# One written order of all steps for a block-sparse attention with a cosine MLP, in place of a planner's priorities

## The chip, the cores and the metric

The kernel runs on one core of a Trainium2 chip. The time is the device time of one launch in microseconds; the median of three runs before the change is 837.22 us (833.31 to 837.58).

## What is computed

```python
def _attn_ref(q, k, v, sampled_blocks):            # q, k, v: (4, 8, 768, 64)
    scores = 1.0 / np.sqrt(D) * np.matmul(q, k.transpose(0, 1, 3, 2))
    mask = np.abs(blk_i - blk_j) <= 1              # blocks of 32 positions, 24 of them
    mask = mask | (blk_i == 0) | (blk_j == 0) | (blk_i == n_blocks - 1) | (blk_j == n_blocks - 1)
    for qb in range(n_blocks):
        for kb in sampled_blocks[qb]:              # three per block of queries
            mask[qb * 32:(qb + 1) * 32, kb * 32:(kb + 1) * 32] = True
    scores = np.where(mask, scores, -1000000000.0)
    attn = np.exp(scores - np.max(scores, axis=-1, keepdims=True))
    attn = attn / (np.sum(attn, axis=-1, keepdims=True) + 1e-09)
    return np.matmul(attn, v).astype(np.float32)

def _moe_ref(x, w_in, w_out):                      # x: 3072 x 512, d_ff 2048
    h = x @ w_in
    return ((h * np.cos(h)) @ w_out).astype(np.float32)
```

The attention's output, its heads side by side, is the x of the second part.

## The kernel before, in words

Work is cut into 24 query tiles of 128 positions, six per batch: five sparse ones (tiles 0 to 4, 6 to 10, 12 to 16, 18 to 22), in which the scores of a pair of heads cover 11 blocks each, and a dense one per batch (tiles 5, 11, 17, 23), which holds the first block and the last three and sees all keys, head by head. Two tiles make one of the 12 blocks of the MLP (block m is fed by tiles 2m and 2m + 1). Every float32 operand is split into a high and a low float16 part, and a product is three multiplications.

One tile goes through these steps, for each pair of heads (or each head of a dense tile): scores on TensorE (L1501, L1502, L1507; dense L1518), eviction with bias and maximum on VectorE (L1534), exponential on ScalarE (L1556), high and low part (ScalarE L1566, VectorE L1570), a transposing DMA of the probabilities that SyncE issues (L1585, PT<-ring; three PT buffers), and the value product on TensorE (L1595, L1607; dense L1621). Then the tile's output is normalised (VectorE L1643), split (L1645, L1647) and transposed by a DMA (L1650, xT<-n). A block of the MLP has, in each of four parts of d_ff, four up steps on TensorE (L1782, 12 multiplications each), evictions on ScalarE (L1791), the reduction of the argument on VectorE (L1801, L1805), the sine on ScalarE (L1809), the product (L1814), its high part (ScalarE L1820) and low part (VectorE L1823), and four down steps on TensorE (L1832, 6 multiplications each). In the first two blocks each part's result is added up on VectorE (L1848). An up or a down step is called an MLP step here. The exponential and the sine stand in different tables of ScalarE, so a change from one to the other is a table load.

Before a batch's first scores, its keys are loaded, squared (ScalarE L1237), reduced to one maximum over all partitions (VectorE L1275, TensorE L1282, VectorE L1285), split (ScalarE and VectorE L1251, L1254) and transposed by DMAs (L1337, W<-kn); its values are split likewise and stored to a scratch in DRAM (L1380), from which each tile's are gathered (SyncE L1460, L1463; GpSimd L1469). Queries are loaded (L1391), split, transposed (L1424) and their halves swapped (L1429, L1431). While the first tiles run, the weights are converted from float64 to float32 (L1693, L1695, L1697) and split (L1737, L1254).

plan_kernel writes down all 3202 steps, each with its engine, a cost, what it reads and writes, and a number pos. In Plan.run of before, a model of the engines, of two DMA queues and of TensorE's clock takes the steps one after the other: of those that could start soonest on an engine it picks the one with the least pos, plus a penalty for a change of table (TSTICK) or of the form of multiplication (MSTICK). A step that needs a new tile (class sp, P, ring, PT and so on, each with 1 to 4 buffers) gets the buffer that comes free soonest by the model. The order in which steps were taken is the order in which they are issued; each engine works through its own instructions in that order, and waits in place where an operand or a buffer isn't there.

Of the kernel before, what the change touches and what calls it, by code (L numbers as in the profile page):

```python
# [62 lines left out]
    -30.456, -29.801, -23.939, -53.034, 166.579, -20.984, 140.138, 219.885, 227.197, 131.714, 120.363, 232.646, -27.188, -24.922, -13.735, -56.138,  # L63
    -94, -55.947, 108.211, -77.198, -23.949, -53.212, -40.157, -72.798, 270.478, 66.707, 68.01, -177.497, 14.041, 28.322, 3.956, 272.798, -299.008,
    78.628, 84.172, -251.907, -2.914, -123.585, 2.465, -91.329, 2.455, 34.414, -267.676, -140.127, -284.431, -284.297, -293.381, -293.391, 192.593,
    9.365, -40.858, -287.926, -293.475, -287.096, 59.248, -394.248, -2.44, -348.918, 17.905, -232.784, 20.189, 100.731, -40.95, -331.99, -113.765,
    -40.634, -367.234, 46.043, -133.846, -367.224, 11.803, 4.97, 24.252, -421.344, 26.722, 28.591, 28.666, -343.265, 24.749, 57.069, 44.723, -158.181,
    36.406, -210.361, -15.746, -343.729, 128.652, -36.656, -371.38, -68.723, 16.426, -352.843, -40.021, 17.512, -383.377, -48.957, -21.419, -347.085,
    -28.841, 56.446, 43.124, 188.518, 11.424, -17.372, 21.646, 33.599, 92.429, 143.48, 196.289, -222.117, -122.398, 8.237, -189.078, -343.107,
    -342.925, 25.279, 10.938, -287.916, -291.521, -287.076, 58.942, 18.504, 18.357, -371.364, -101.311, -423.627, 74.946, -15.912, -13.582, 41.721,  # L70
    -245.857, -245.911, -244.196, -43.279, -222.107, -87.019, -399.291, -65.977, -134.438, 46.449, 60.7, 33.135, 4.468, 123.512, 268.427, 33.261,
    -248.251, -248.261, 212.998, -102.21, 48.096, 13.762, -106.375, -119.619, -147.859, -108.524, -207.38, 26.503, 77.242, -59.055, 1.603, 67.419,
    -87.097, -106.365, 67.989, -37.319, -59.065, 69.972, 72.05, -154.526, 55.53, -154.393, -169.552, 56.724, -229.085, -231.809, 74.109, 141.111,
    110.575, 115.939, -212.079, 38.276, 59.016, -125.91, 76.35, 74.089, 148.617, 164.638, -161.055, 83.947, 111.93, 81.411, 76.871, -59.456, -83.696,
    159.259, 85.519, 93.411, 17.344, 71.116, 184.532, 68.131, 74.808, 107.885, 77.651, 84.302, 130.956, 28.443, 113.94, 76.784, 109.173, 89.802,
    -45.113, 117.791, 159.783, 68.413, -124.822, -171.216, 43.388, 0.239, 17.471, -215.269, 120.448, 241.879, 122.369, 97.725, 62.454, 170.072,
    164.502, -7.94, -4.787, 2.973, -52.72, 223.723, 122.511, -117.03, -107.768, 171.807, 166.99, 31.038, -64.944, 122.176, -107.825, 122.166, 239.2,
    144.286, 112.315, 156.325, 382.871, 80.018, 71.115, -102.354, 162.701, -80.093, 79.039, -102.344, 99.128, 128.496, 58.997, -8.015, 105.462,
    35.675, -49.533, 145.181, 119.619, -28.145, 93.292, 142.357, 308.89, 128.763, 119.724, 117.514, 85.487, 85.477, 353, 135.215, 147.675, 191.49,
    174.352, -36.186, -36.871, -123.396, 176.099, -39.179, 309.094, -39.029, 132.778, 148.258, 163.293, -175.451, 70.065, 131.553, 172.196, -210.132,  # L80
    188.27, 242.828, 164.956, 160.647, -62.194, -92.423, 244.643, 165.526, -39.019, -40.767, -44.622, 45.727, 174.671, 176.081, 274.008, 148.864,
    212.867, -21.454, 198.526, 93.467, 88.563, 186.068, 198.293, 45.786, 47.752, -3.729, -25.778, -197.69, -62.453, -353.585, -65.75, -397.087, 40.03,
    -58.957, 41.172, 22.215, 6.449, 26.152, -152.555, 116.726, 144.461, 85.242, 267.182, -72.696, 32.61, -223.053, -234.241, -274.177, 88.133,
    -142.875, 36.777, -48.023, -48.508, -27.185, 36.777, -102.2, -105.699, -69.594, -75.188, -107.644, -166.721, 44.732, 50.054, 8.787, 37.825,
    -105.709, -42.273, -82.868, 10.422, -134.435, -66.455, 34.062, 91.891, 21.079, 56.89, -51.579, -9.933, 68.144, 253.555, -66.358, -348.47, 48.572,
    3.193, -182.808, -147.869, -130.834, 67.487, -210.07, 70.849, 1.538, 69.097, -108.251, 51.995, 60.727, -206.919, 14.069, -202.843, -210.687,
# [171 lines left out]
    604.774, 824.955, 1051.126, 942.72, 677.48, 454.761, 798.868, 681.849, 454.538, 686.552, 852.787, 839.193, 954.833, 823.585, 684.874, 898.166,  # L258
    688.133, 688.922, 863.203, 684.355, 688.932, 564.474, 873.725, 773.958, 800.794, 591.607, 799.478, 678.833, 688.123, 848.093, 681.039, 688.123,
    748.898, 735.298, 810.843, 809.183, 742.566, 703.148, 722.615, 732.095, 700.957, 675.385, 798.996, 569.188, 736.375, 735.308, 760.316, 655.823,  # L260
    635.618,
]


# [1649 lines left out]
```

## Time and profile before

| | |
|---|---|
| median of three runs | 837.22 us |
| profiled execution, its own time | 824.2 us |
| its span | 822.4 us |
| TensorE (PE) busy | 719.6 us, 87% |
| VectorE (DVE) busy | 641.1 us, 78% |
| ScalarE (ACT) busy | 635.7 us, 77% |
| GpSimd (POOL) busy | 107.4 us, 13% |
| mean granted TensorE clock | 0.938 |

Busy shares are averages over the whole span. The page cuts the span into 40 slices of 20.6 us, and a digit there is the busy share of one slice in tenths; PEclk is the granted clock of TensorE in the same way. The time between the span and the execution's own time is 1.8 us.

### The profile page before, as it was taken

The page shows a single profiled execution, that of the slowest core. Times are in us where ns is not written, and L with a number is a line of the kernel's source. Part 1 is how long each engine was busy: PE and PEld are TensorE (multiplying, and loading weights), DVE is VectorE, ACT ScalarE, POOL GpSimd, SP SyncE. Part 2 cuts the span into 40 slices and gives each one's busy share as a digit, 9 for nine tenths or more (in the row PEclk, how much of TensorE's full clock was granted, in tenths as well). Part 3 has the DMA queues.
Part 4 walks back from the last instruction along what each step waited for, and adds up shares of the span by engine and source line. Part 5 has one row for each costly group of instructions (what it writes and reads, how often), then busy time and mean ns, then how long its engine had stood idle before and what let it go on. Part 6 is the DMA issues. An engine that isn't in the chain of part 4 may idle for free.

```text
span 822.4 us, 23028 instructions
## 1 busy us (share of the span) xinstructions
PE 719.6 (87%) x9272; PEld 507.2 (62%) x9272; DVE 641.1 (78%) x1617; ACT 635.7 (77%) x1218; POOL 107.4 (13%) x128
## 2 busy tenths in 40 slices
PE   3537589899889856999999979999999979999998
PEld 2425467566466435767767647767586558577573
DVE  5979999999969763889878975989768957967362
ACT  3667899899868973999969985989679967977251
POOL 6232203000022022100030212000300210200000
PEclk9955689999899986999999998999999989999999
DMA  8999977954989899999997999978977997675100
GB/s 309 325 236 259 239 150 174 212 126 113 205 257 183 157 196 167 171 228 177 270 187 158 178 207 206 202 154 186 217 140 134 196 181 163 157 130 99 26 26 26
DMA packets 270299, 146.55 MB, mean 178 GB/s; under 512 B 241648, under 2 KB 241776, under 8 KB 270192
## 3 DMA queue, kind: packets, MB, share of 16 engines
q1 hardware_dynamic: 265072, 129.35, 74.3%
q0 software_dynamic: 5120, 15.73, 8.6%
q8 instruction: 72, 1.18, 0.6%
q14 instruction: 35, 0.29, 0.1%
HBM read 68.23 MB, written 12.58 MB: 98 GB/s over the span
## 4 chain that ended last, share of the span: by engine, by line
PE 37%; ACT 14%; DMA 13%; DVE 9%; issue 3%; SPq 1%; DVEq 0%; ACTq 0%
PE ph L1782 15%; PE po L1832 14%; DMA PT<-ring 7%; ACT P L1556 4%; PE xp L1607 2%; ACT ring L1566 2%; DMA W<-kn 2%; DMA scr<-n 2%; PE sp L1518 1%; DVE P L1534 1%; DMA qs<-in_q_dram 1%; ACT hs L1791 1%; DVE g L1823 1%; ACT junk L1237 1%; PE xp L1595 1%
## 5 line engine op out<-in xcount | busy, mean ns | idle before, releaser
L1782 PE MATMUL ph<-xT,w 128*128 128x256 f16 x2304 | 272.3, 277 | 8.3 <-ACT hs L1791 4.2
L1832 PE MATMUL po<-w,g 128*128 128x512 f16 x1152 | 265.6, 381 | 4.1 <-DVE kn L1848 1.6
L1782 PEld LDWEIGHTS <-w 128*128 128x128 f16 x2304 | 225.6, 99 | 45.6 <-issue 8.5
L1832 PEld LDWEIGHTS <-g 128*128 128x128 f16 x1152 | 108.7, 98 | 124.4 <-issue 4.1
L1556 ACT ACTIVATE P<-P,sm 128x352 f32<-128x352 f32 (+1 forms) x224 | 152.0, 680 | 32.3 <-DVE sm L1551 23.0
L1469 POOL DMA_INDIRECT V<-scr,gidx x80 | 91.8, 1147 | 595.0 <-PE xp L1595 278.2
L1570 DVE TENSOR_TENSOR ring<-P,ring 128x704 f16<-128x704 f32 (+1 forms) x112 | 100.5, 906 | 23.8 <-ACT ring L1566 22.7
L1534 DVE CUSTOM_DVE_ANT_1 P<-sp,bias 128x352 f32<-128x352 f32 x160 | 78.6, 519 | 35.4 <-PE sp L1507 35.1
L1791 ACT ACTIVATE hs<-ph,sm 128x512 f32<-128x512 f32 x96 | 63.0, 677 | 44.7 <-PE ph L1782 40.8
L1566 ACT CAST ring<-P 128x704 f16<-128x704 f32 (+1 forms) x112 | 86.5, 786 | 13.3 <-DMA PT<-ring 12.7
L1814 DVE SCALAR_TENSOR_TENSOR hs<-hs,sm,g 128x1024 f32<-128x1024 f32 x48 | 61.1, 1281 | 11.8 <-ACT g L1809 11.2
L1501 PE MATMUL sp<-W,U 128*128 128x192 f16 x320 | 52.5, 265 | 13.5 <-DVE sm L1534 10.7
L1823 DVE TENSOR_TENSOR g<-hs,g 128x1024 f16<-128x1024 f32 x48 | 58.6, 1223 | 6.9 <-ACT g L1820 6.8
L1809 ACT ACTIVATE g<-g,sm 128x1024 f32<-128x1024 f32 x48 | 54.7, 1145 | 11.5 <-DVE g L1805 11.2
L1595 PE MATMUL xp<-V,PT 96*32 96x64 f16 x1920 | 30.9, 203 | 35.4 <-DMA PT<-ring 35.4
L1805 DVE SCALAR_TENSOR_TENSOR g<-g,hs 128x1024 f32<-128x1024 f32 x48 | 58.3, 1218 | 0.6 <-DVE Wg L1343 0.2
L1820 ACT ACTIVATE g<-hs 128x1024 f16<-128x1024 f32 x48 | 50.4, 1051 | 8.4 <-DVE hs L1814 7.9
L1801 DVE TENSOR_SCALAR g<-hs 128x1024 f32<-128x1024 f32 x48 | 32.9, 690 | 28.0 <-ACT hs L1791 27.9
L1595 PEld LDWEIGHTS <-PT 96*32 96x32 f16 x1920 | 21.7, 102 | 51.7 <-DMA PT<-ring 43.5
L1502 PE MATMUL sp<-W,U 128*128 128x64 f16 x320 | 47.8, 205 | 0.0
L1607 PE MATMUL xp<-V,PT 128*128 128x64 f16 x960 | 46.6, 204 | 0.0
L1502 PEld LDWEIGHTS <-U 128*128 128x128 f16 x320 | 33.1, 104 | 15.5 <-issue 12.1
(164 smaller groups left out, 919.1 us busy)
## 6 DMA issues: line engine op xcount, KB each, us to landing
V<-scr SPq DMA_DIRECT2D x20, 384.0 KB, 5.1
stage<-in_k_dram SPq DMA_DIRECT2D x12, 512.0 KB
w<-in_moe_w_in_dram SPq DMA_DIRECT2D x12, 512.0 KB, 6.9
w<-in_moe_w_out_dram SPq DMA_DIRECT2D x12, 512.0 KB, 4.4
V<-scr SPq DMA_DIRECT2D x8, 768.0 KB, 6.3
scr<-n SPq DMA_DIRECT2D x21, 256.0 KB, 3.3
qs<-in_q_dram SPq DMA_DIRECT2D x20, 256.0 KB, 3.5
U<-U SPq DMA_DIRECT2D x40, 128.0 KB, 2.9
```

The lines of the kernel that those rows point to most:

```text
L1469: self.nc.gpsimd.indirect_dma_start(V[:96, 2 + j, :], None, self.scr[b][:, :], bass.IndirectOffsetOnAxis(ap=self.gidx[:96, c : c + 1], axi ...
L1502: mm(spv[:, :, 96:128].rearrange("p y (n c) -> p y n c", c=hf), u, ends, start=False, stop=False)
L1534: self.nc.vector.tensor_tensor_reduce(out=self.p_view(n, Pt)[:, a].rearrange("p (n c) -> p n c", c=hf), in0=sp[:, :w].rearrange("p (n c) - ...
L1556: self.nc.scalar.activation(Pv[:, a], Pv[:, a], AF.Exp, scale=qc[:, 4:5], bias=nb[:, bcol : bcol + 1], accum_out=sums[:, 2 * j + a : 2 * j ...
L1566: self.nc.scalar.copy(R[:, :, 0, : self.width(n)], self.p_view(n, Pt))
L1570: self.nc.vector.tensor_tensor(R[:, :, 1, :w], self.p_view(n, Pt), R[:, :, 0, :w], ALU.subtract)
L1607: mm(xp[:, h, :], PT[:, 6 * a + 3 * l + c, :], V[:, c, h, d0:d1], start=False, stop=(a == 1 and c == 1 and x == len(terms) - 1),)
L1782: self.nc.tensor.matmul(ph[:, ff, :], self.W1[p][:, wl, cc, c * P : (c + 1) * P], xT[:, xl * NCC + cc, :], start=(j == 0), stop=(j == len( ...
L1791: self.nc.scalar.activation(hs[:, h * 512 : h * 512 + 512], ph.rearrange("p f t -> p (f t)"), AF.Copy, scale=self.turns[b][:, p : p + 1])
L1814: self.nc.vector.scalar_tensor_tensor(hs, hs, c[:, p : p + 1], kt, op0=ALU.mult, op1=ALU.mult)
L1823: self.nc.vector.tensor_tensor(g[:, 1024:2048], hs, g[:, 0:1024], ALU.subtract)
L1832: self.nc.tensor.matmul(po, g[:, gl, ff, t * P : (t + 1) * P], self.W2[p][:, wl, ff, :], start=(first and ff == half * hf and j == 0), sto ...
```

## The change

The table POS holds a place in one total order for each of the 3202 steps (the whole numbers 0 to 3201) where it held priorities. Plan.run sorts the steps by it and issues them so, and no longer models times: ArrayClock and Queues are gone. A step's new tile gets a buffer that was never used, or else, of those whose last user already stands in the order, the one whose last use stands farthest back. The steps, their instructions and the number of buffers stay. Places in code behind the table differ by line only: a line of the changed kernel is the old one less 213 (L1432 was L1645).

```diff
 POS = [
-    -30.456, -29.801, -23.939, -53.034, 166.579, -20.984, 140.138, 219.885, 227.197, 131.714, 120.363, 232.646, -27.188, -24.922, -13.735, -56.138,
...
+    1, 11, 22, 12, 262, 52, 14, 3, 15, 80, 21, 105, 4, 17, 16, 18, 13, 29, 30, 31, 32, 33, 35, 37, 115, 323, 252, 40, 148, 92, 307, 609, 347, 179,
...
 ]
@@ Plan
-    def run(self, delta, stick, mstick=0.0):
...
-            for eng, cand in ready.items():
-                at = max(free[eng], dma.ends[0] - 1.75) if eng == "SP" else free[eng]
...
-                    key = (o.pos + (stick if o.table and o.table != table else 0.0) + (mstick if eng == "PE" and o.mode[0] != mode else 0.0), o.n)
...
-            for v in o.acq:
-                v.avail, v.slot = slot_time(v)
-                v.t = self.classes[v.cls][v.slot]
...
+    def run(self):
+        order = sorted(self.ops, key=lambda o: (o.pos, o.n))
+        for v in {id(v): v for o in order for v in o.acq}.values():
+            v.left, v.freed = len(v.ops), 0
             for o in v.ops:
                 o.vals.append(v)
         holder = {c: [None] * len(t) for c, t in self.classes.items()}
+        done = set()
+        for k, o in enumerate(order):
+            assert all(id(p) in done for p in o.preds | {v.ops[0] for v in o.held}), o.name
             for v in o.acq:
+                h = holder[v.cls]
+                free = [x for x in range(len(h)) if h[x] is None] or [x for x in range(len(h)) if not h[x].left]
+                x = min(free, key=lambda x: h[x].freed if h[x] else x)
+                h[x], v.t = v, self.classes[v.cls][x]
             for v in o.vals:
                 v.left -= 1
+                v.freed = k
+            done.add(id(o))
         self.order = order
@@ block_sparse_attention_then_cos_mlp
-    pl.run(PARAMS["DELTA"], PARAMS["TSTICK"], PARAMS["MSTICK"])
+    pl.run()
```

First piece: VectorE, where the keys of batch 1 are split and the first scores (tile 6, rows with bias) are evicted. kn is the split key, stage the loaded one, g and hs belong to block 2 of the MLP. Before:

```order
L1254 SCALAR_TENSOR_TENSOR kn1_89<-stage2_80,sm_77,kn1_89 128x4x64
L1254 SCALAR_TENSOR_TENSOR kn0_88<-stage1_79,sm_77,kn0_88 128x4x64
L1801 TENSOR_SCALAR g0_84<-hs1_83 128x1024
L1254 SCALAR_TENSOR_TENSOR kn1_89<-stage2_80,sm_77,kn1_89 128x4x64
L1805 SCALAR_TENSOR_TENSOR g0_84<-g0_84,hs1_83 128x1024
L1534 ISA P2_98,sm_77<-sp0_115,bias_74 128x352
L1534 ISA sm_77 128x1
L1534 ISA P2_98,sm_77<-sp0_115,bias_74 128x352
L1534 ISA sm_77 128x1
L1823 TENSOR_TENSOR g2_86<-hs0_82,g2_86 128x1024
L1551 TENSOR_SCALAR sm_77<-sm_77 128x2
```

After:

```order
L1041 SCALAR_TENSOR_TENSOR kn0_88<-stage3_81,sm_77,kn0_88 128x4x64 x2
L1321 ISA P2_98,sm_77<-sp0_115,bias_74 128x352
L1321 ISA sm_77 128x1
L1321 ISA P2_98,sm_77<-sp0_115,bias_74 128x352
L1321 ISA sm_77 128x1
L1338 TENSOR_SCALAR sm_77<-sm_77 128x2
L1041 SCALAR_TENSOR_TENSOR kn1_89<-stage1_79,sm_77,kn1_89 128x4x64
L1588 TENSOR_SCALAR g3_87<-hs1_83 128x1024
L1035 RECIPROCAL sm_77<-sm_77 128x1
L1321 ISA P0_96,sm_77<-sp0_115,bias_74 128x352
L1321 ISA sm_77 128x1
```

Before, the argument of block 2's fourth and last part (L1801, L1805) stood in front of the first score; now the scores come first and the third part's (L1588) behind them, with two splits of keys.

Second piece: ScalarE, at tile 7 of batch 1. ring is a high part of probabilities, P the exponentials. Before:

```order
L1556 ACTIVATE P1_97,sm_77<-P1_97,sm_77 128x352 x2
L1820 ACTIVATE g0_84<-hs1_83 128x1024
L1566 CAST ring1_101<-P1_97 128x2x352
L1556 ACTIVATE P2_98,sm_77<-P2_98,sm_77 128x352 x2
L1237 ACTIVATE junk_72,sm_77<-stage1_79 128x512
L1566 CAST ring0_100<-P2_98 128x2x352
L1237 ACTIVATE junk_72,sm_77<-stage1_79 128x512
L1556 ACTIVATE P0_96,sm_77<-P0_96,sm_77 128x352 x2
```

After:

```order
L1343 ACTIVATE P3_99,sm_77<-P3_99,sm_77 128x352
L1343 ACTIVATE P2_98,sm_77<-P2_98,sm_77 128x352
L1353 CAST ring1_101<-P3_99 128x2x352
L1024 ACTIVATE junk_72,sm_77<-stage2_80 128x512
L1343 ACTIVATE P2_98,sm_77<-P2_98,sm_77 128x352
L1607 ACTIVATE g3_87<-hs1_83 128x1024
L1343 ACTIVATE P0_96,sm_77<-P0_96,sm_77 128x352
L1578 ACTIVATE hs0_82<-ph0_118,sm_77 128x512
L1343 ACTIVATE P0_96,sm_77<-P0_96,sm_77 128x352
```

Before, the high part of block 2's last part (L1820) came just ahead of tile 7's exponentials and closed the block on this engine; now that of the third part (L1607) and the eviction of the fourth part's up steps (L1578) stand among them.

Third piece: SyncE, from the last transpose of tile 7's probabilities on (U is a transposed query, qs a loaded one, n a tile's output or query before its transpose). Before:

```order
L1585 DMA_TRANSPOSE PT2_105<-ring0_100 128x12x128
L1463 DMA V1_107<-scr1_123 16x2048
L1650 DMA_TRANSPOSE xT0_109<-n162_92 128x8x128
L1585 DMA_TRANSPOSE PT0_103<-ring2_102 128x12x128
L1431 DMA U1_95<-U1_95 64x1024
L1429 DMA U1_95<-U1_95 64x1024
L1585 DMA_TRANSPOSE PT1_104<-ring1_101 128x12x128
L1585 DMA_TRANSPOSE PT2_105<-ring0_100 128x12x128
L1650 DMA_TRANSPOSE xT0_109<-n160_90 128x8x128
L1585 DMA_TRANSPOSE PT0_103<-ring2_102 128x12x128
```

After:

```order
L1372 DMA_TRANSPOSE PT1_104<-ring0_100 128x12x128
L1178 DMA qs0_93<-in_q_dram 96x512
L1178 DMA qs0_93<-in_q_dram 32x512
L1250 DMA V0_106<-scr1_123 16x2048
L1211 DMA_TRANSPOSE U0_94<-n160_90 128x8x128
L1372 DMA_TRANSPOSE PT2_105<-ring2_102 128x12x128
L1437 DMA_TRANSPOSE xT1_110<-n161_91 128x8x128
L1372 DMA_TRANSPOSE PT0_103<-ring1_101 128x12x128
L1437 DMA_TRANSPOSE xT1_110<-n162_92 128x8x128
L1218 DMA U0_94<-U0_94 64x1024
L1216 DMA U0_94<-U0_94 64x1024
L1372 DMA_TRANSPOSE PT1_104<-ring0_100 128x12x128
```

The second xT row is tile 7's output, which block 3 waits for: three transposes of tile 8's probabilities were ahead of it, and two are now, but also the query of tile 11 (L1178) and the transposed query of tile 10 (L1211).

## Rows read from the trace of the kernel before

**Rows 1.** The page, 40 slices of the span: PE busy and granted clock, in tenths.

```profile
PE   3537589899889856999999979999999979999998
...
PEclk9955689999899986999999998999999989999999
```

**Rows 2.** Busy us by stretch: PE, PEld, DVE, ACT, POOL; granted clock, DMA share, GB/s.

```profile
40.00:120.00 80.00, 48.73 (x980) 38.91 (x980) 72.46 (x191) 63.13 (x134) 17.03 (x15) 0.68 0.98 223
120.00:226.00 106.00, 98.22 (x1078) 67.13 (x1078) 103.37 (x239) 94.80 (x172) 7.74 (x4) 0.94 0.76 166
226.00:270.00 44.00, 41.00 (x324) 28.28 (x324) 33.06 (x75) 31.44 (x62) 9.31 (x8) 1.00 0.91 223
270.00:322.00 52.00, 31.94 (x728) 21.48 (x727) 33.29 (x121) 36.61 (x93) 7.64 (x8) 0.79 1.04 169
322.00:470.00 148.00, 146.84 (x1862) 105.09 (x1860) 124.27 (x314) 132.79 (x255) 16.14 (x15) 0.99 0.94 194
470.00:499.00 29.00, 22.63 (x473) 14.54 (x472) 20.43 (x81) 23.80 (x58) 6.32 (x7) 0.93 1.17 211
499.00:650.00 151.00, 149.65 (x1822) 105.89 (x1820) 121.55 (x305) 124.96 (x233) 16.07 (x16) 0.99 0.87 179
650.00:673.00 23.00, 17.84 (x364) 11.50 (x354) 17.35 (x60) 18.38 (x47) 4.04 (x4) 0.91 1.07 173
```

**Rows 3.** Waits of PE (us, times, longest) in 270:322, 470:499, 650:673.

```profile
PE xp L1595 <- DMA PT<-ring: 12.2, 6, 3.1
...
PE xp L1595 <- DMA PT<-ring: 6.4, 3, 3.7
...
PE xp L1595 <- DMA PT<-ring: 4.3, 2, 3.5
```

**Rows 4.** Timeline of DVE, 226 to 243 us: start, us, instruction, [idle before].

```profile
238.10 0.16 DVE L1275 TENSOR_REDUCE sm<-sm 128x1 bf16<-128x6 f32 x1 [3.29 <-ACT junk L1237]
239.86 0.15 DVE L1242 TENSOR_SCALAR sm<-sm 128x1 int32<-128x1 int32 x1 [1.60 <-ACT n L1237]
```

**Rows 5.** The chain that ended last, in order of time: start, us, what.

```profile
322.24 2.29 PE ph L1782 x12
...
552.16 1.29 PE po L1832 x6
...
565.54 1.31 PE ph L1782 x12
```

**Rows 6.** Groups of DVE by form: count, busy us, mean ns, idle before.

```profile
L1814 DVE SCALAR_TENSOR_TENSOR hs<-hs,sm,g 128x1024 f32<-128x1024 f32 x48 | 61.1, 1281 | 11.8 <-ACT g L1809 11.2
L1823 DVE TENSOR_TENSOR g<-hs,g 128x1024 f16<-128x1024 f32 x48 | 58.6, 1223 | 6.9 <-ACT g L1820 6.8
L1805 DVE SCALAR_TENSOR_TENSOR g<-g,hs 128x1024 f32<-128x1024 f32 x48 | 58.3, 1218 | 0.6 <-DVE Wg L1343 0.2
...
L1801 DVE TENSOR_SCALAR g<-hs 128x1024 f32<-128x1024 f32 x48 | 32.9, 690 | 28.0 <-ACT hs L1791 27.9
...
L1254 DVE SCALAR_TENSOR_TENSOR kn<-stage,sm,kn 128x256 f16<-128x256 f32 x36 | 16.4, 480 | 8.1 <-ACT kn L1251 8.1
```

**Rows 7.** Timeline of ACT around one table load.

```profile
336.62 1.28 ACT L1809 ACT_TABLE_LOAD   x1
337.92 1.15 ACT L1809 ACTIVATE g<-g,sm 128x1024 f32<-128x1024 f32 x1
```

**Rows 8.** Timelines of PE: tile 5 to block 2, tile 11's scores, tile 23.

```profile
224.38 1.21 PE L1621 MATMUL xp<-V,PT 128*128 128x64 f16 x36
...
233.19 5.40 PE L1782 MATMUL ph<-xT,w 128*128 128x256 f16 x48
...
358.19 0.81 PE L1518 MATMUL sp<-W,U 128*128 128x384 f16 x4
...
760.42 0.69 PE L1621 MATMUL xp<-V,PT 128*128 128x64 f16 x18
760.94 13.12 PE L1832 MATMUL po<-w,g 128*128 128x512 f16 x60
```

More of the change, by code (lines that the diff above doesn't have):

```diff
@@ L277, in __init__ @@
     def __init__(self, cls=None, t=None):
-        self.cls, self.t, self.slot, self.avail = cls, t, None, 0.0
+        self.cls, self.t = cls, t
         self.ops = []
@@ L351, in op @@
         o.preds, o.succ, o.acq, o.held, o.n = set(after), [], [], [], len(self.ops)
-        o.start = o.end = o.done = None
+        o.vals = []
         for key, writes in [(k, False) for k in r] + [(k, True) for k in w]:
@@ L375, in op @@
         return o
-    def run(self, delta, stick, mstick=0.0):
-        ops = self.ops
-        queues = {c: collections.deque() for c in self.classes}
-        for o in sorted(ops, key=lambda o: (o.pos, o.n)):
-            for v in o.acq:
-                queues[v.cls].append(v)
-        heads = {q[0] for q in queues.values() if q}
-        for o in ops:
-            before = sorted(o.preds | {v.ops[0] for v in o.held}, key=lambda x: x.n)
-            o.need = len(before) + sum(v not in heads for v in o.acq)
-            for p in before:
-                p.succ.append(o)
-            o.vals = []
-        for v in {id(v): v for o in ops for v in o.acq}.values():
-            v.left, v.free_at = len(v.ops), 0.0
+    def run(self):
+        order = sorted(self.ops, key=lambda o: (o.pos, o.n))
+        for v in {id(v): v for o in order for v in o.acq}.values():
+            v.left, v.freed = len(v.ops), 0
             for o in v.ops:
@@ L394, in run @@
         holder = {c: [None] * len(t) for c, t in self.classes.items()}
-        ready = {"SP": [], "PE": [], "DVE": [], "ACT": [], "POOL": []}
-        free = dict.fromkeys(ready, 0.6)
-        dma, table, order, clock = Queues(), None, [], ArrayClock()
-        def ready_now(o):
-            t = 0.0
-            for v in o.held:
-                t = max(t, v.avail)
-            for p in o.preds:
-                t = max(t, p.done if p.dma or p.eng == o.eng == "PE" else p.done + LAT[p.eng])
-            o.floor = t
-            ready[o.eng].append(o)
@@ L492, in run @@
-            for x in o.succ:
-                x.need -= 1
-                if not x.need:
-                    ready_now(x)
+                v.freed = k
+            done.add(id(o))
         self.order = order
-        return max(o.done for o in order)
 def plan_kernel(env, B, H, S, D, DM, DFF, pr):
```

104 lines of the change are left out of this document (removed), and 323 rows, old and new, of the table POS.

## The prediction

> **What bounds the kernel now.** I read the page first, for where TensorE (PE) rests and where its clock falls [rows 1]: before about 120 us, in two or three slices near 300 us, in one near 490 and one near 670. Then the busy time by stretch [rows 2]. From 40 to 226 us VectorE (DVE) is the limit: 72.46 of 80 and 103.37 of 106 us. From 322 us on PE is: it rests 1.2 us of the 148 from 322 to 470 and 1.4 us of the 151 from 499 to 650. Between these lie the places where a new batch begins: 270 to 322 (PE idle 52.00 - 31.94 = 20.1 us, granted clock 0.79, so partly on the lower, 1.2 GHz level), 470 to 499 (idle 6.4) and 650 to 673 (idle 5.2). Third, the waits of PE in these three [rows 3]: 12.2, 6.4 and 4.3 us are waits of a value product for the transposed probabilities (PT<-ring). PE executes in its written order, so each wait also holds whatever multiplications stand behind it. Last, DVE at the first of these places [rows 4]: it rests 3.3 and 1.6 us before the maxima of the new keys, the first for squares on ScalarE (ACT), the second for the scale of a query.
>
> The kernel ends when PE has done its multiplications. In the stretches where PE is full, an order can save nothing; it can save in the first 226 us if DVE rests less, and at the three places if other multiplications are at hand or the attention starts sooner.
>
> **The change, part by part.** The steps and their instructions are the same 3202; only their order and the buffer each gets are new. All durations below are of the one profiled execution, 824.2 us (span 822.4), which lies 1.6% under the median of 837.22; the sum is made against 824.2, and its ratio is carried over to the median.
>
> *A, up to 226 us.* DVE idles 7.5 us from 40 to 120 and 2.6 from 120 to 226 [rows 2]; that is the most a better order could win while DVE is the limit. Ahead of the normalisation of tile 1, which the first MLP block waits for, the new order takes two splits of weights away on DVE and puts conversions of loads 18, 24, 26 and 27 and two score evictions there: about as much work as it takes away. So little is won: between 0 and 10.1 us, nearer the small end, 3.
>
> *B, the first new batch (226 to 322).* On DVE the first score eviction of tile 6 now stands in front of one L1814 (1.28), one L1823 (1.22), two L1805 (1.22 each), two L1801 (0.69 each) and two splits of keys at L1254 (0.48 each) [rows 6] that it stood behind: 1.28 + 1.22 + 2.44 + 1.38 + 0.96 = 7.3 us that it need not wait for (first piece of the order). On PE ten MLP steps of 1.3 us (twelve L1782 or six L1832 multiplications [rows 5]) move behind the first scores of tile 6. Nine steps of the second projection of block 2 now stand between the first scores of tile 8 and the first step of block 3, where none stood (ACT's piece shows the same block's work among the exponentials). On SP the transpose of tile 7's output, which block 3 waits for, goes ahead of two more transposes of probabilities, not one (third piece). The gain is bounded by 0, if the transfers set the end of this stretch, and by the 20.1 us that PE idles. I take the 7.3 us, and half of the 4.9 us that DVE idled before the keys' maxima [rows 4], since the splits of V now begin earlier among DVE's work: 7.3 + 2.4 = 9.7. The slower clock in this stretch is inside that, because PE is not its limit.
>
> *C, the second (470 to 499).* The 6.4 us are three waits for probabilities [rows 3]. Between the scores of head pair 2 of tile 14 and their value product stood 5 MLP steps; now 13 do, 10 us more cover. That covers the wait wherever the probabilities come no later than now. The lower clock cost 22.63 x 0.07 = 1.6 us. But ahead of the first step of block 6 four small pieces (scores and value products, some 0.7 us each; a dense value product takes 0.6 [rows 8]) are gone against one MLP step more, which gives 2.8 - 1.3 = 1.5 back. 0 to 8.0, I take 5 + 1.6 - 1.5 = 5.1.
>
> *D, the third (650 to 673).* The same: 5.2 us idle, 17.84 x 0.09 = 1.6 us of lower clock; 21 MLP steps stand between pair 1 of tile 20 and its value product, where 7 did. 0 to 6.8, I take 4 + 1.6 = 5.6.
>
> *E, table loads.* ACT switches between exponential and sine 48 times, not 42: six loads of 1.28 us [rows 7], 7.7 us of ACT. From 322 to 470 ACT is busy 132.79 of 148 us [rows 2], so 15 us stand free beside PE; that covers them, and if it were gone all 7.7 would count. I take 1. In the trace the sine starts at 337.92, right after a load from 336.62 to 337.90 [rows 7], with nothing more behind the load. The Trainium skill (ScalarE: Activation LUTs, What ACT_TABLE_LOAD costs) has a drain of about 1380 ns with every load, 2.66 us in all; by it, an estimate, the six would take 16 us, just over ACT's slack there, and the sum would be about 1 us worse. The load agrees with the trace, the drain does not show there.
>
> *F, first steps of the MLP blocks.* Between the last value product a block needs and its first step lies a chain: normalise, split, transpose. Unhidden it took 233.19 - 225.59 = 7.6 us; at the last block PE had ten steps of 13.1 us in its place [rows 8]. The new order leaves one MLP step less there at block 1 (1.3 us), two less and three heads' scores (0.81 each [rows 8]) at block 4 (5.0) and two less at block 11 (2.6): 0 to 8.9 us lost. I take the last block's 2.6, because no other work is left there, and nothing at block 4, where 6 MLP steps (7.8 us) and more remain.
>
> Slots in turn, and more waits written as instructions of their own: both without a row of their own; each changes which earlier reader a step waits for, and the bounds of B to D hold them. I take 0.
>
> Sum: -3.0 - 9.7 - 5.1 - 5.6 + 1.0 + 2.6 = -19.8; 824.2 - 19.8 = 804.4 us, 2.4% less; of the median, 837.22 x 804.4/824.2 = **817 us**. Its own range is about 805 to 831.
>
> **The rivals.**
> *All the idle time goes.* With A's 10.1, B's 20.1, C's 8.0 and D's 6.8 the time is 824.2 - 45.0 = 779.2, of the median 792 us. For it: the waits in all three places are of one kind, and the added cover (10 to 18 us) is far above each. Against: block 3 still waits for tile 7, whose chain has the same length.
> *The transfers set the pace.* From 270 to 322 the DMA share is 1.04 and from 470 to 499 it is 1.17, the highest of the table [rows 2], and the waits there are all on DMAs [rows 3]. The bytes are the same. If transposes come no sooner, B to D win nothing, and -3.0 + 1.0 + 2.6 = +0.6: 824.8, of the median 838 us. Against: the share is 0.91 from 226 to 270 and 0.87 from 499 to 650, so there is room to start sooner. The Trainium skill (DMA: Bandwidth & Descriptors, Issuing engines are not separate DMA queues) says that all issuers share the same 16 engines and interleave; by that rule this rival has the upper hand wherever the share is over 1, and the trace agrees that transfers are late there.
> *The wait moves to the first MLP step (slower).* PE has used up cover for its value products that it formerly had in front of the blocks. If the chain of F takes 13 us, as long as the cover at the last block was, rather than 7.6, the new order waits at the first steps of blocks 1, 4 and 11 for all of 8.9 us, and the waits of B to D come back there: -3.0 + 1.0 + 8.9 = +6.9, 831.1, of the median 844 us. It decides once the first step could start no sooner than about 10 us behind the last value product, the cover that is left at blocks 4 and 11. For: SP is in order, and loads for later tiles (queries of tile 11, transposed query of tile 10) now go ahead of tile 7's output. Against: tile 7's output is itself ahead of more probabilities than before.
>
> **How the numbers follow.** Forecast 0.60, all idle gone 0.18, transfers set the pace 0.12, moved wait 0.10. A measurement of this kernel tells about 0.5%, 4 us, from no change. The first two are faster by more than that, 0.78; the third is no change, 0.12; the last slower, 0.10. The range leaves out about half of the second case and the last: 793 to 840.
>
> **What would show it.** Right: in the new profile PE's idle time between the end of block 2 and the first step of block 3 falls by about 10 us and that step starts some 10 to 13 us sooner (it was at 322.24 us [rows 5]); waits of value products for PT<-ring at the three places fall from 22.9 us in all to under 10; the two later dips of the clock are gone; before 120 us little differs. Wrong: the stretch around the new batches has the same PE idle under another name (a wait of the first step of a block for xT), or PE idles within 322 to 470 or 499 to 650, or ACT ends waits of PE in these.

## The result and the profile after

The changed kernel takes 842.49 us, the median of five runs (839.04 to 850.09); the kernel before took 834.39 beside it (829.79 to 837.58). The ratio is 1.014 [1.009, 1.019]: 1.4% **slower**, where 2.4% faster was forecast. The change was traced in an execution of 839.04 us (span 836.9, mean granted clock 0.934).

The page's slices of PE and of its granted clock, as in [rows 1]:

```profile
PE   4435687988898978899989889999989989999998
...
PEclk9656688999999999999989989999999999999999
```

The dip of PE near 300 us has shrunk, as expected: its slices of 5 and 6 are now 7 and 8. But from the 17th slice on (335 us), where PE had stood at 9 in all but three slices, seven slices now stand at 8. The same windows as in [rows 2], with the same columns:

```profile
40.00:120.00 80.00, 46.02 (x813) 36.93 (x813) 66.08 (x186) 58.04 (x126) 16.34 (x16) 0.64 0.92 223
120.00:226.00 106.00, 88.64 (x1096) 62.02 (x1094) 92.56 (x210) 89.01 (x164) 5.08 (x4) 0.92 0.73 159
226.00:270.00 44.00, 41.66 (x388) 28.01 (x386) 39.84 (x96) 36.64 (x70) 9.85 (x8) 1.00 1.02 224
270.00:322.00 52.00, 43.19 (x787) 27.16 (x786) 41.21 (x142) 43.92 (x98) 8.57 (x8) 0.97 1.09 197
322.00:470.00 148.00, 141.35 (x1820) 100.46 (x1817) 118.77 (x308) 128.07 (x251) 14.76 (x14) 0.97 0.93 192
470.00:499.00 29.00, 22.99 (x375) 13.91 (x373) 18.27 (x54) 24.19 (x51) 5.94 (x7) 0.88 1.08 194
499.00:650.00 151.00, 146.34 (x1925) 105.31 (x1923) 122.59 (x315) 125.84 (x241) 15.87 (x14) 1.00 0.91 172
650.00:673.00 23.00, 18.86 (x259) 10.55 (x259) 17.05 (x50) 20.45 (x41) 6.21 (x7) 1.00 0.94 195
```

Four things differ. From 120 to 226 us DVE is busy for 92.56 us and no longer 103.37. From 270 to 322 PE works 11 us more. From 322 to 470 it rests 6.65 us where it had rested 1.2, and from 499 to 650 4.66 where it had rested 1.4. At 470 it rests as much as before. The waits of PE over the whole span answer to [rows 3]; first those of before:

```profile
PE xp L1595 <- DMA PT<-ring: 35.4, 16, 5.9
PE sp L1501 <- DVE sm L1534: 10.7, 9, 3.2
```

and those of the change:

```profile
PE sp L1288 <- DVE sm L1321: 24.8, 12, 4.6
PE sp L1305 <- DVE sm L1321: 14.4, 8, 4.1
PE xp L1382 <- DMA PT<-ring: 8.8, 5, 2.9
```

The waits for transposed probabilities did go: 35.4 us in 16 waits over the span before, 8.8 in 5 now. In their place PE waits for the score buffer, which VectorE's eviction (L1321, was L1534) has to empty: 39.2 us, where that took 10.7. So the question is why evictions come late. The trace of one of them, at the first score of batch 2 (tile 12), in the order of time and over all engines:

```profile
421.13 0.92 POOL L1256 DMA_INDIRECT V<-scr,gidx  x1 [79.78 <-DMA W<-kn]
...
424.52 0.35 PE L1294 MATMUL sp<-Wg,U 128*32 128x96 f16 x16
...
424.80 0.92 POOL L1256 DMA_INDIRECT V<-scr,gidx  x1 [0.30 <-issue]
...
425.64 1.23 DVE L1592 SCALAR_TENSOR_TENSOR g<-g,hs 128x1024 f32<-128x1024 f32 x1
...
429.71 1.04 PE L1619 MATMUL po<-w,g 128*128 128x512 f16 x4 [0.34 <-issue]
...
430.42 0.92 POOL L1256 DMA_INDIRECT V<-scr,gidx  x1 [0.30 <-issue]
...
432.63 0.52 DVE L1321 CUSTOM_DVE_ANT_1 P<-sp,bias 128x352 f32<-128x352 f32 x1 [5.76 <-remote]
...
433.66 0.32 PE L1288 MATMUL sp<-W,U 128*128 128x192 f16 x1 [2.91 <-DVE sm L1321]
```

GpSimd issues eight gathers of sampled V rows one behind the other (L1256, was L1469; one every 1.2 us) from 421.13 to 431.3. The score's last multiplication ends inside that group, at 424.87. DVE is free at 426.87, yet it starts the eviction only at 432.63. The chain of waits puts the 5.73 us between down to "another core or an unknown queue", that is, to no instruction it knows: the signal that the score is done is recorded at 432.60, 7.7 us after the end and 1.3 us after the end of the group's last gather (431.34). The profile models the ends of multiplications, but PE runs in order and had started the next ones from 424.80 on, so the score was done long before. PE, whose next scores need that buffer, then rests 2.91 us. I call such a signal **late** if the next signal on record comes over 0.6 us after the end of the multiplication that gives it. The change's trace has 28 late signals, 72.8 us in all, every one inside a group of gathers; the traced execution of before had 2 (5.4 us). This count is too high, since some records are missing inside the groups (439 for the 443 multiplications that signal in the change), and then a later one is taken: for five of the 28, the instruction that reads the result had started before the record. So I also count the places where a reader that had been idle for over 0.15 us starts within 0.15 us of a late signal, as here, and call them **held**, with the smaller of its idle time and the lateness: 13 in the change (28.9 us), none in the traced execution of before. Only signals of PE hold anybody. By the first rule 40 signals of DVE and 38 of ACT are late in the change as well, but no idle engine starts with one of them: there it is the record that is missing or late.

The Trainium skill (SBUF — State Buffer, Who interferes with whom) says that a VectorE instruction with two SBUF inputs contends with a GpSimd instruction that reads SBUF, and that PE and ACT wait for nobody. By that rule L1592, with two SBUF inputs, should be the one that suffers here; it ran 1.23 us inside the group, as before [rows 6], and it was PE's signal that came late. So the rule does not explain this wait.

The granted clock falls during the rest and stays low behind it. Windows of 2 us, same columns as above:

```profile
430.00:432.00 2.00, 0.74 (x4) 0.23 (x3) 0.00 (x0) 0.00 (x0) 1.03 (x2) 1.00 1.26 203
432.00:434.00 2.00, 0.34 (x4) 0.32 (x4) 1.37 (x9) 0.00 (x0) 0.00 (x0) 0.54 1.23 198
434.00:436.00 2.00, 2.00 (x28) 1.40 (x26) 1.96 (x6) 1.90 (x2) 0.00 (x0) 0.50 0.91 131
436.00:438.00 2.00, 2.00 (x11) 1.38 (x10) 1.89 (x5) 1.83 (x4) 0.00 (x0) 0.50 1.05 173
438.00:440.00 2.00, 2.00 (x15) 1.64 (x14) 1.62 (x10) 1.25 (x5) 0.00 (x0) 0.76 1.15 308
```

After the rest of 2.91 us the granted clock is 0.54, 0.50, 0.50 and 0.76 for four windows, the 1.2 GHz level, with PE busy throughout the last three. That is 2 x (0.46 + 0.50 + 0.50 + 0.24) = 3.4 us more, of which 0.9 at most fall in the window in which it still rested.

### The profile page after: what moved, and what is told of

Same layout as the page of the kernel before. It is cut to its first block, busy times and chain, and to the rows that moved or that the text cites. A ratio compares the mean times of both kernels' runs of the same rounds, so it can differ in the third digit from the quotient of the medians.

```text
span 836.9 us, 23088 instructions
## 1 busy us (share of the span) xinstructions
PE 723.4 (86%) x9272; PEld 504.7 (60%) x9272; DVE 640.5 (77%) x1617; ACT 644.1 (77%) x1224; POOL 106.4 (13%) x128
## 4 chain that ended last, share of the span: by engine, by line
PE 50%; DVE 20%; ACT 12%; DMA 9%; issue 6%; another core or an unknown queue 2%; SPq 1%; DVEq 0%; ACTq 0%
PE po L1619 19%; PE ph L1569 19%; DMA PT<-ring 4%; DVE P L1321 4%; DVE ring L1357 3%; ACT P L1343 2%; PE xp L1394 2%; PE sp L1288 2%; DVE g L1592 2%; PE sp L1305 2%; DMA qs<-in_q_dram 2%; PE sp L1294 2%; PE xp L1408 2%; DVE hs L1601 1%
## 5 line engine op out<-in xcount | busy, mean ns | idle before, releaser
L1569 PE MATMUL ph<-xT,w 128*128 128x256 f16 x2304 | 276.6, 276 | 8.7 <-DMA xT<-n 3.2
L1619 PE MATMUL po<-w,g 128*128 128x512 f16 x1152 | 274.9, 387 | 0.8 <-issue 0.8
L1569 PEld LDWEIGHTS <-w 128*128 128x128 f16 x2304 | 223.6, 99 | 50.3 <-issue 10.3
L1619 PEld LDWEIGHTS <-g 128*128 128x128 f16 x1152 | 110.6, 99 | 119.4 <-issue 9.8
L1256 POOL DMA_INDIRECT V<-scr,gidx x80 | 87.1, 1089 | 582.9 <-PE xp L1382 265.7
L1321 DVE CUSTOM_DVE_ANT_1 P<-sp,bias 128x352 f32<-128x352 f32 x160 | 79.1, 519 | 58.3 <-PE sp L1294 33.6
L1578 ACT ACTIVATE hs<-ph,sm 128x512 f32<-128x512 f32 x96 | 63.7, 676 | 32.6 <-PE ph L1569 26.8
L1607 ACT ACTIVATE g<-hs 128x1024 f16<-128x1024 f32 x48 | 50.2, 1048 | 13.6 <-DVE hs L1601 13.6
L1592 DVE SCALAR_TENSOR_TENSOR g<-g,hs 128x1024 f32<-128x1024 f32 x48 | 58.5, 1219 | 0.7
L1588 DVE TENSOR_SCALAR g<-hs 128x1024 f32<-128x1024 f32 x48 | 33.0, 687 | 18.7 <-ACT hs L1578 17.9
L1321 DVE CUSTOM_DVE_ANT_1 P<-sp,dbias 128x384 f32<-128x384 f32 x64 | 34.3, 552 | 15.5 <-PE sp L1305 14.6
```

The source lines that it names most:

```text
L1256: self.nc.gpsimd.indirect_dma_start(V[:96, 2 + j, :], None, self.scr[b][:, :], bass.IndirectOffsetOnAxis(ap=self.gidx[:96, c : c + 1], axi ...
L1321: self.nc.vector.tensor_tensor_reduce(out=self.p_view(n, Pt)[:, a].rearrange("p (n c) -> p n c", c=hf), in0=sp[:, :w].rearrange("p (n c) - ...
L1569: self.nc.tensor.matmul(ph[:, ff, :], self.W1[p][:, wl, cc, c * P : (c + 1) * P], xT[:, xl * NCC + cc, :], start=(j == 0), stop=(j == len( ...
L1578: self.nc.scalar.activation(hs[:, h * 512 : h * 512 + 512], ph.rearrange("p f t -> p (f t)"), AF.Copy, scale=self.turns[b][:, p : p + 1])
L1592: self.nc.vector.scalar_tensor_tensor(kt, kt, MAGIC, hs, op0=ALU.subtract, op1=ALU.subtract)
L1619: self.nc.tensor.matmul(po, g[:, gl, ff, t * P : (t + 1) * P], self.W2[p][:, wl, ff, :], start=(first and ff == half * hf and j == 0), sto ...
```

## The experiments

Theory G (from the trace above): the order itself is no loss; it sets GpSimd's groups of gathers where PE's signals and the transposes have to pass, and that costs more than it saves. Rivals: the slots handed out in turn cost it; a certain stretch of the order costs it; DVE and the scores take turns badly whatever GpSimd does.

### Slots, and which stretch

e1 keeps the new slot rule and gives each step its rank in the order that the planner had issued before. e2 to e4 join the two orders at a time: e2 is the new order up to 322 us and then that of before, e3 the reverse, e4 as e3 with the join at 226 us. Of the table, two pieces are shown; e1 takes both, e2 the second alone, e3 and e4 the first alone.

```diff
 POS = [
-    1, 11, 22, 12, 262, 52, 14, 3,
+    1, 9, 15, 12, 18, 11, 2, 3,
...
-    1650, 1663, 1634, 1635, 1654, 1616, 1644, 1670,
+    1659, 1663, 1633, 1639, 1661, 1666, 1672, 1678,
```

> The order of before, step for step, written as a table; only the buffers are handed out in turn. If the slots cost the time (theory slots), it stands about 8 us above before, near 842 us of a before of 834. If the order does (theories early order and late order), it is within 4 us of before.

> Steps that the changed kernel had started by 322 us stand in its order, the rest in the order of before. By the two traces both kernels have done the same multiplications at 322 us (0.2 us apart, each counted at its usual duration), while the new one was 18 us behind at 226. Late order (the time is lost behind 322 us): within 4 us of before, 834. Early order (work put off in the first 226 us is missing to the end): near 842.

> The counterpart: before's order for what it had started by 322 us, then the new order. Late order: 842 to 849, as slow as the whole change or more, since the ledger shows 14 to 16 us lost from 322 us to the end. Early order: within 4 us of before, 834.

> Before's order until 226 us, then the new one, which keeps the new order around the first new batch (226 to 322 us), where the new kernel caught up 18 us. If that gain stands by itself and only the late part loses 14 to 16 us: 830 to 834. If it was only the work put off before 226 us that filled the idle time, there is nothing to fill it with here: 845 to 850, as in the run that is cut at 322 us.

| | median us | ratio to before |
|---|---|---|
| e1 order of before, slots in turn | 829.94 | 0.997 [0.993, 1.001] |
| e2 new order up to 322 us | 833.68 | 1.003 [0.999, 1.007] |
| e3 new order from 322 us | 847.55 | 1.019 [1.012, 1.027] |
| e4 new order from 226 us | 841.30 | 1.013 [1.006, 1.020] |

The slots cost nothing. With the gathers in, the first 322 us of the new order neither win nor lose; the loss lies behind them. At a join some steps had to move back for want of a buffer, so e3's extra 0.5% is not read as a part of the change.

### The same two kernels traced again

e5 and e6 change nothing.

> The kernel before, unchanged, for a second trace of the same program. In the trace that the prediction was made from, a score's end and the eviction that waits for it are never over 1 us apart without another reason; in the run of the old order with slots in turn, completions of TensorE that fall inside a group of value gathers on GpSimd are up to several us late (30 of them). Theory held signals (it differs from execution to execution of one program): 15 to 35 late completions here and 828 to 837 us. Theory slots or order: 2 again, as in the first trace.

> The changed kernel, unchanged, for a second trace and on the same chip as the next two runs. 838 to 846 us; held signals: some 20 to 30 late completions again, at places that differ in part.

The kernel before took 834.24 us in the second trace (span 832.5), the change 842.62 (840.5; its median 845.08, ratio 1.015 [1.009, 1.020]). So the execution of 824.2 us on which the prediction stood was an unusual one (19 others, taken beside e1 to e4, lie between 826.45 and 837.74). What made it so is seen at one place, tile 9's last pair. In the first trace (GpSimd, PE, DVE):

```profile
327.57 0.92 POOL L1469 DMA_INDIRECT V<-scr,gidx  x1 [0.30 <-issue]
327.58 0.35 PE L1507 MATMUL sp<-Wg,U 128*32 128x96 f16 x16
...
328.19 0.53 DVE L1534 CUSTOM_DVE_ANT_1 P<-sp,bias 128x352 f32<-128x352 f32 x1 [0.84 <-PE sp L1507]
```

and in the second, e5:

```profile
333.18 0.92 POOL L1469 DMA_INDIRECT V<-scr,gidx  x1 [0.30 <-issue]
333.19 0.35 PE L1507 MATMUL sp<-Wg,U 128*32 128x96 f16 x16
...
335.63 0.92 POOL L1469 DMA_INDIRECT V<-scr,gidx  x1 [0.30 <-issue]
337.67 0.53 DVE L1534 CUSTOM_DVE_ANT_1 P<-sp,bias 128x352 f32<-128x352 f32 x1 [4.71 <-PE ph L1782]
```

Same program, same gathers, same place: once the eviction starts 0.26 us behind the score, once 4.1. The profile puts e5's wait down to a later step (L1782), because three signals come together there: PE's signalling multiplications end at 333.55 (the score), 334.96 and 336.27, and their signals are recorded at 337.64, 337.77 and 337.90. A group of gathers can hold a signal, but need not. Late signals: 2 and 20 in the two traces of before, 30 in e1's, 28 and 25 in the two of the change (e6: 78.0 us). Held readers: none and 9 (20.1 us) in the two traces of before, 11 (18.5 us) in e1's, 13 (28.9 us) and 14 (35.6 us) in the two of the change. By count alone the two orders hardly differ; they differ in which signals are hit, and the new order's holds are longer. Among its longest is the first score of a batch (tile 12: 7.7 us late, and 7.88 in e6), on which a whole batch hangs.

### Without gathers, or with other loads in their place

In e7 and e8 SyncE loads fixed rows of V, in e9 and e10 GpSimd does, so the sampled values are not the ones asked for. All 80 gathers are replaced (the expectation of e7 says 72):

```diff
-        self.nc.gpsimd.indirect_dma_start(
-            V[:96, 2 + j, :],
-            None,
-            self.scr[b][:, :],
-            bass.IndirectOffsetOnAxis(ap=self.gidx[:96, c : c + 1], axis=0),
-        )
+        self.nc.sync.dma_start(V[:96, 2 + j, :], self.scr[b][96 * j : 96 * j + 96, :])
```

```diff
-        self.nc.gpsimd.indirect_dma_start(
...
+        self.nc.gpsimd.dma_start(V[:96, 2 + j, :], self.scr[b][96 * j : 96 * j + 96, :])
```

In e15 and e16 nothing is loaded there, and the two V buffers are zeroed once:

```diff
-        self.nc.gpsimd.indirect_dma_start(
...
+        if n < 2 and (n, 0) not in self.blank:
+            self.blank.add((n, 0))
+            self.nc.gpsimd.memset(V[:96, 2:6, :], 0.0)
```

> The old order (slots in turn), with the 72 gathers of the sampled value blocks replaced by plain loads of as many bytes from fixed rows, issued by SyncE, so that GpSimd issues no gathers; the sampled rows of V are not the ones asked for. Held signals: no late completions, and about the time of the one trace that had none, 820 to 826 us. Theory that gathers do not matter: 828 to 834, or more for 72 more issues on SyncE.

> The same replacement in the changed kernel. If the new order is slower because its scores fall into the gathers: within 4 us of the run before this one. If the order itself loses its 10 us behind 322 us: 10 us above it, 830 to 836. Theory that gathers do not matter: 842.

> The old order with each gather replaced by one plain load of as many bytes from fixed rows, issued by GpSimd as the gather was (the sampled rows of V are not the ones asked for). It tells whether any load that GpSimd issues holds the signals, or the gather with its list of rows. If any load does: within 4 us of before, 830 to 836, and late completions in its groups. If the list does: as with SyncE's loads, 805 to 812, and none late.

> The same in the new order. With SyncE's loads the new order stood 6 us above the old one, and its trace had one wait for a value load (3.3 us, with the clock at 0.77 behind it) that SyncE's own queue had made late. Theory that the new order only loses by the gathers' holds: within 3 us of the run before this one. Theory late order: 6 to 10 us above it.

> The old order with the 80 gathers left out and nothing in their place (the sampled rows of V stay what was there before). It gives the old order's time without GpSimd's gathers, their held signals and their 15.7 MB. With SyncE's loads in their place it was 807; without those 800 to 808.

> The same in the new order. Theory that the order by itself is better, as predicted (18 to 20 us), and the gathers covered it: 780 to 790. Theory that the two orders are worth the same and differ only in what the gathers do to them: within 4 us of the run before this one. Theory late order: 6 us and more above it.

Ratios to the kernel before, with the late signals of one trace of each (by the first rule):

| sampled rows of V | order of before | late | new order | late |
|---|---|---|---|---|
| gathered by GpSimd (before and e1; change, e6) | 1, 0.997 | 2, 20; 30 | 1.014, 1.015 | 28; 25 |
| plain loads by GpSimd (e9, e10) | 0.994 [0.990, 0.998] | 0 | 1.000 [0.995, 1.004] | 0 |
| plain loads by SyncE (e7, e8) | 0.967 [0.962, 0.972] | 0 | 0.975 [0.970, 0.979] | 0 |
| none (e15, e16) | 0.967 [0.962, 0.971] | 0 | 0.954 [0.949, 0.959] | 0 |

**With no gathers the new order is the faster one**: 788.1 against 799.5 us, 11.4 us (1.4%). Only there is the order tried with neither gathers nor loads in their place. The gathers, with the data that they load, cost the old order 827.13 - 799.5 = 27.6 us and the new one some (1.0145 - 0.9543) x 830 = 50; the difference, 22, is twice what the order gains. That settles the sign. It does not follow that the late signals alone make the loss: with plain loads in their place, and none late, the new order still stands behind the old one, by 6 us (e8, e7) and 5 us (e10, e9; the intervals of these two ratios just overlap).

Plain loads on GpSimd, with no late signal in either trace, still cost 18 us against none in the traced executions of the old order (817.25 against 798.98) and 31 in those of the new (823.02 against 791.88); by the medians it is 0.027 and 0.045 of the time. The first trace of before, in which no reader was held, also lies 25 us above e15's (824.2 against 798.98). So late signals are not the whole price of the groups. e10 shows another part. In the stretch from 390 to 440 us the transfers (KB each, median us from issue to landing) were

```profile
V<-scr POOLq DMA_DIRECT2D x8, 192.0 KB, 4.9
...
xT<-n SPq DMA_TRANSPOSE x1, 11.0
```

and PE waited for that transpose, with its clock at 0.82 to 0.84 from 410 to 430 us:

```profile
PE ph L1564 <- DMA xT<-n: 6.2, 1, 6.2
```

The transpose that feeds an MLP block was issued among the eight V loads, at 407.20 us with six of them ahead of it, and took 11.0 us, where the transposes of new keys (W<-kn) in that stretch have a median of 4.8. The last two V loads took 10.3 each. That the loads made it late is read from this one place. The Trainium skill (DMA: Bandwidth & Descriptors, Issuing engines are not separate DMA queues) says that all issuers share the same 16 engines and interleave; the trace agrees, with its 11.0 us against 4.8 beside the other issuer's loads. How the rest of e9's price comes about stays open.

e8 lies 6 us above e7: behind SyncE's other transfers, one V load came late at 685 to 700 us, with PE's wait of

```profile
PE xp L1377 <- DMA V<-scr: 3.4, 2, 3.3
```

and a granted clock of 0.77 there, worth 15 x 0.23 = 3.4 us. In this one trace the two add up to the 6 us.

### Gathers set behind the first scores

These load all that the kernel loads. A gather that the table SIG names waits for an exponential: GpSimd first copies one element of that exponential's row sum, which the exponential's step keeps in sig. In e12 and e17 some gathers also stand later in the order than before.

```diff
+        if (n, j) in SIG:
+            self.nc.gpsimd.tensor_copy(self.tick, self.sig[SIG[n, j]])
...
+        self.sig[n, j, a] = sums[0:1, 2 * j + a : 2 * j + a + 1]
```

> The new order, complete, in which 49 of the 80 gathers first wait for an exponential (GpSimd copies one element of its row sum ahead of the gather), so that they no longer run in groups of four and eight, and the eight of each new batch come behind the first scores, not among them. Held signals lasting to the end of a group: late completions shorter (most under 2 us, none of 5 to 8 us), and 6 to 12 us less than the change, 831 to 838. Theory that the holds cost nothing beside the order: 842 or more.

> The old order, complete, with as many gathers (49 of 80) made to wait for an exponential as in the run of the new order that has them apart (807.7 us); 38 of them stand later in GpSimd's order than before. If the two orders are worth the same and the new one only lost more by held signals: 803 to 812. If the new order is better by itself, as the prediction had it, and the holds covered that up: 815 to 826, the time of the executions of before that had hardly a held signal.

> The new order with only the gathers of the first two tiles of batches 1 to 3 apart (18 of them), so that the groups of eight no longer lie on the first scores of tiles 6, 12 and 18; the groups of four stay. Of the 35 us that all 49 brought, the late completions at the eights (3 places, 7.7, 3.4 and 2.2 us, with the slow clock behind them) explain 10 to 18: 824 to 832.

> The counterpart: only the 31 gathers of the other tiles apart, the eights of the new batches left in groups. If the two parts add up to 35 us: 817 to 825.

> The old order, complete, with only the gathers of the later tiles of each batch apart (28), the eights left where they were: there they lie on multiplications of the MLP, which no score waits for. The new order gained some 14 us from its 31. If the old order, too, is held mostly in its fours: 814 to 820. If it is not: 826 to 830.

| | gathers that wait | median us | ratio | late |
|---|---|---|---|---|
| e11 new order | 49 | 807.65 | 0.977 [0.969, 0.985] | 1 |
| e13 new order, eights alone | 18 | 839.59 | 1.013 [1.008, 1.018] | 33 |
| e14 new order, fours alone | 31 | 828.70 | 0.997 [0.994, 1.000] | 27 |
| e12 order of before | 49 | 825.85 | 0.995 [0.992, 0.998] | 21 |
| e17 order of before, fours | 28 | 816.17 | 0.985 [0.980, 0.991] | 3 |

**e11 beats both kernels**: 807.65 us, 0.037 of the time under the change and 21 us under the kernel before beside it. Its slices of PE and clock have neither the dips of [rows 1] nor those of the change:

```profile
PE   3446597978899888999999998999999999999997
...
PEclk9655788989999998999999999999999999999999
```

e13 and e14 are misses: each frees one kind of group and should have won its share, but against the change's 1.014 the shares are -0.001 and -0.017 where both together are -0.037, and late signals stay at 33 and 27 (11 and 9 held readers, 20.0 and 15.2 us; none in e11 and e17). The two kinds do not act one by one. e17 shows that the old order is relieved in the same way, by half of what it wins without any gathers (0.985, 0.967). e12 says little: 21 signals were late and 4 readers held (9.3 us), though its gathers are spread about as widely as e11's. In e12 seven follow one another from 438.9 to 449.1 us, and there a score's reader was held for 5.0 us. In e11, too, seven gathers (of tiles 12 and 13) still follow one another by 1.3 to 2.0 us, with a copy between, but from 428.55 us on, behind tile 12's first exponential, and there none was held. So it is not shown which of three things helps: the later moment, the gap, or the copy. Nor is it shown what holds a signal.

## Why the prediction was wrong

To size its terms without the ends of the run, I count the work that PE has done by a given time: each step at the median of its own durations, once finished. Records overlap, so only differences between orders mean something. With gathers these are means of two traces (e1 and e5; the change and e6), without them e15 and e16:

| PE's work, us, by | old, gathers | new, gathers | new - old | old, none | new, none | new - old |
|---|---|---|---|---|---|---|
| 322 us | 241.8 | 242.8 | +1.0 | 254.9 | 263.0 | +8.1 |
| 470 | 403.4 | 399.5 | -3.9 | 424.2 | 428.0 | +3.8 |
| 499 | 426.3 | 421.9 | -4.4 | 452.6 | 460.8 | +8.2 |
| 650 | 590.8 | 587.2 | -3.6 | 623.3 | 634.2 | +10.9 |
| 673 | 615.4 | 608.5 | -6.9 | 648.4 | 660.1 | +11.7 |
| 774 | 725.5 | 718.9 | -6.6 | 765.8 | 773.1 | +7.3 |

From here on a term is read as the step from one row to the next. The last column's lead of 7.3 us is close to the 7.1 us by which e16's span is shorter (789.9 against 797.0), and the lag of 6.6 with gathers to the 6.1 us between the mean spans (838.7 against 832.65). Between the two, the gathers take 7.1 us of lead up to 322, 4.9 at the second new batch and 4.1 at the third, just where the prediction expected its gains.

**The step that failed** is the opening of the change's parts: it costs MLP steps, transfers and table loads, and has no term for GpSimd's gathers. They stand in the same order, the change moves them against the scores, and [rows 2] had POOL at 4 to 17 us in each stretch, which no term took up. Beside it stands its base: "All durations below are of the one profiled execution, 824.2 us". That execution had no held reader where another of the same program had 9, so the part of the cost that comes from held signals was not in the rows that it was worked out from.

**"In the stretches where PE is full, an order can save nothing."** It can lose there: from 322 to 470 us the new order falls back by 4.9 us with gathers and 4.3 without. The work that it holds back for the starts of batches is worked off at the very end.

**A, -3.** Wrong in sign. At 226 us e16 has 159.6 us of work done and e15 169.0, so the new order is 9.4 behind. The windows of e15 (first fence) and e16 show it:

```profile
120.00:226.00 106.00, 96.94 (x1082) 65.25 (x1081) 103.51 (x239) 94.17 (x172) 0.00 (x0) 0.98 0.72 158
...
270.00:322.00 52.00, 41.67 (x863) 30.72 (x861) 38.42 (x136) 43.20 (x109) 0.00 (x0) 0.84 0.97 163
...
470.00:499.00 29.00, 25.96 (x592) 21.13 (x575) 20.82 (x69) 23.75 (x55) 0.00 (x0) 1.00 1.03 167
```

```profile
120.00:226.00 106.00, 90.30 (x1040) 61.13 (x1037) 93.02 (x205) 88.56 (x161) 0.00 (x0) 0.92 0.75 154
...
270.00:322.00 52.00, 47.94 (x941) 34.63 (x939) 44.83 (x145) 51.00 (x111) 0.00 (x0) 1.00 1.15 192
...
470.00:499.00 29.00, 28.45 (x497) 21.06 (x495) 25.39 (x70) 27.49 (x56) 0.00 (x0) 1.00 0.97 159
```

DVE, the limit there, rests 13.0 us in the new order and 2.5 in the old; the change itself has 13.4. The score halves of the dense tile 5 and their evictions take turns over the one score buffer: in the change PE waits 10.0 us for L1321 there, and DVE 6.8 for the scores of L1305. It is work put off, as the next term shows.

**B, -9.7.** From 226 to 322 us e16 makes up 17.5 us, the 9.4 and 8.1 more: 8.1 for A and B together, 12.7 predicted. PE is at 47.94 of 52 us and full clock there. With gathers 1.0 is left. The mark given for it failed: block 3's first step starts at 322.78 us in the change and at 322.24 before [rows 5]; without gathers at 305.29 instead of 310.27, 5 us sooner and not 10 to 13. Of the other marks, the waits for probabilities fell as said (8.8 us in the whole span, where under 10 were expected at the three places). The dip of the clock at 650 to 673 us is gone (1.00), that at 470 to 499 is not (0.88).

**C, -5.1, was right without gathers**: +4.4 us. With them it is -0.5. **D, -5.6**, was too large: +0.8, since e15 has no idle time left at 650 to 673 us to be saved; with gathers it is -3.3. The first trace's rests in D, 5.2 us, thus went with the gathers, as did most of its waits for probabilities: without gathers the old order has 11.9 us of these over the whole span, not 35.4.

**E, +1, and the slots, 0:** e1 bears out the slots, and among PE's waits in the change, those for ACT are 4.0 us or less on any line, and none points to the six table loads. **F, +2.6:** from 673 to 774 us the order loses 4.4 without gathers; block 11 is last either way, and more work is left for then.

The waits moved, as the text's last paragraph allowed for, but not where it looked. In e15 (first) and e16 the longest kinds of wait over PE's scores and value products are

```profile
PE sp L1285 <- DVE sm L1318: 11.9, 11, 2.7
PE xp L1379 <- DMA PT<-ring: 11.9, 9, 2.5
```

```profile
PE sp L1285 <- DVE sm L1318: 21.3, 10, 4.5
PE sp L1302 <- DVE sm L1318: 15.1, 9, 4.5
```

With no gathers at all, the new order exchanges 11.9 us of waits for transposes for 24.5 us more of waits for the score buffer (36.4 against 11.9). So the rival that DVE and the scores take turns badly is true as well, and it goes with a gain of 1.4% without gathers where 2.4% was forecast; but by itself it does not make the loss.

Of the prediction's rivals, "transfers set the pace" and "the wait moves to the first MLP step" gave 838 and 844 us, near the 842.49 found, but for other reasons: waits of first MLP steps for xT come to 3.2 us in the whole change (`PE ph L1569 <- DMA xT<-n` in its list of waits), and the transfers' share at 270 to 322 us, 1.09, did not keep PE from working 11 us more.

## What to carry to other kernels

Before an order is costed, take a second trace of the kernel as it stands: where two executions of one program differ by 1%, the rows of the lucky one leave out a cost. When steps are moved, list what every engine that issues DMAs does at that moment, also one that is 13% busy; a wait that the chain gives to "an unknown queue" while another engine issues a group of gathers is worth a trial without these gathers. And two orders are compared fairly only with the disturbance taken away: here the better order was the slower kernel until its gathers were set behind the first scores.

## What the hardware showed that I had not expected

A completion signal of TensorE can reach its reader up to 7.9 us after the multiplication's end while GpSimd issues indirect gathers one behind the other, in some executions and not in others (no reader held, and 9, in two executions of one program). With plain loads on GpSimd, loads on SyncE or none, not one was late in the traces. The 80 gathers occupy GpSimd for 87.1 us in the change, yet with the data that they load they cost it some 50 us of its time. After a rest of 2.91 us PE worked for some 5 us on the 1.2 GHz level (granted 0.50, 0.50, 0.76 in windows of 2 us), so that the rest cost nearly twice its length.
